# The second layer's matmul groups held in written order, with thirds of the output product between products of one PSUM bank

## The chip, the cores and the metric

The kernel runs on one core of a Trainium2 chip. The metric is the device time of one execution in microseconds (us). A core has five engines that run side by side, each with its own queue of instructions: TensorE (PE in the profile, its weight loads PEld), VectorE (DVE), ScalarE (ACT), GpSimd (POOL) and SyncE (SP), which here issues the DMAs. Matmuls write to PSUM, which is divided into banks; VectorE and ScalarE read the results there.

## The reference, cut to what matters

The whole program is an attention over packed keys and two feed-forward layers. The change touches the second layer alone:

```
g = x @ w_gate                       # x: 4608 x 512, w_gate: 512 x 1536
silu = g * (1 / (1 + exp(-g)))
val = x @ w_val                      # w_val: 512 x 1536
out = (silu * val) @ w_out           # w_out: 1536 x 512
```

All of it is in 32-bit floats; the kernel multiplies in the format float32r and takes three matmuls in place of one.

## The kernel before, in words

**Three matmuls for one.** Every operand is split into a high part and a low part. The helper `mm3` (line 284) adds low x high (line 287), high x high (line 288) and high x low (line 289) into one PSUM bank. So all of the matmuls in question carry these three line numbers, and the tile names tell them apart.

**Tiling of the second layer.** The 4608 tokens are cut into six blocks of 768 (`s`), each of two halves of 384 (`t`). The 1536 inner columns are cut into twelve pieces (`f`). One step `n` does one piece for one block, `n = 12 s + f`, so there are 72 steps. Within a step the two halves of gate and value (four blocks of results) come from seven products in place of eight, in Strassen's manner (`product`, line 894, `k` = 0 to 6). Each takes a sum or difference of input blocks (`xs2`, tiles `xA` and `xS`) against one of weight blocks (`gvw`, tile `gv`), with two `mm3` of 384 columns: six matmuls.

**The banks.** `gv_step` (line 913) uses the tags `h` and `at`, each with two banks: product 0 and 2 go to `xb`, 1, 3 and 5 to `yb`, 4 and 6 to `vb`. Products 0 and 2 add up in one bank, as do 4 and 6, and 1, 3 and 5; between them an engine reads the bank as it then stands. Line 928 copies product 0 to `p1` on ScalarE; `add` (line 911, VectorE) forms `u2`, `u3` and a new `p1`. Lines 932 and 933 make silu for half t=0 (ScalarE, VectorE); lines 948 and 949 make it for half t=1 (ScalarE, GpSimd). Lines 952 (VectorE, t=0) and 954 (GpSimd, t=1) multiply by the value.

**The output product.** `halves` (line 971) splits each result into `ph` (ScalarE, line 973) and `pl` (GpSimd, line 975). `out_unit(n, t)` (line 980) multiplies them by a piece of `w_out`. It does so in three groups of 128 tokens (`g`), each one `mm3` of 512 columns into a bank of its own: three matmuls, a third of the unit. Six banks (`acc0` to `acc3`, one of `h`, one of `at`) gather the output over the twelve steps of a block, which leaves `xb` with `vb`, and all `yb`, one bank each for most of a block. The first matmul of each third takes `pl` as its weights, the other two `ph`. At f = 11 the six banks are copied out (lines 995 and 997) and sent to memory, through a buffer that is also the buffer of the sums of the next block's inputs (`sums_x`, line 826, and `split_x`, line 835).

**What sets the order.** The kernel is written as one sequence; in it `out_unit` of step n-1 is called from within step n, through `between(0)` ahead of product 4 and `between(1)` at the step's end. The language's scheduler then runs through a simulated timeline and queues, on each engine, whatever is ready first by its own costs; where two are ready, what is written earlier. Dependences on tiles and banks are kept by semaphores. So the order of PE's queue before the change is the scheduler's, not that of the text. `tc.issue_after(ins)` (already used in lines 211, 630 and 635, outside of this layer) makes every instruction traced inside it, on the engine of `ins`, stand behind `ins` in that engine's queue; it adds no semaphore.

**Block changes.** In the last step of a block the inputs of the next are split into high and low parts (ScalarE line 856, VectorE lines 857, 840 and 846); loads (line 816), sums (lines 832 and 833) and the weight loads `load_gv` (line 873, SP) are hoisted by the scheduler as early as their buffers allow.

Of the kernel before, what the change touches and what calls it, by code (L numbers as in the profile page):

```python
# [8 lines left out]
F32 = mybir.dt.float32  # L9
F32R = mybir.dt.float32r  # L10
U32 = mybir.dt.uint32
AF = mybir.ActivationFunctionType
# [5 lines left out]
P = 128  # L18
T = 384
# [82 lines left out]
def tile_kernel(  # L102
# [21 lines left out]
    nc = tc.nc  # L124
    B, H, S, D = q.shape
    NP = p.shape[2]
    NT, DM = out.shape
    KC = DM // P
    NF1 = alpha.shape[0] // P
    NF2 = w_out2.shape[0] // P  # L130
# [6 lines left out]
    NBLK = NT // (2 * T)  # L137
# [4 lines left out]
    ps = ctx.enter_context(tc.tile_pool(name="ps", bufs=1, space=PSUM))  # L142
# [3 lines left out]
    vp = ctx.enter_context(tc.tile_pool(name="v", bufs=1))  # L146
# [137 lines left out]
    def mm3(o, wts, xs, start, stop, **kw):  # L284
        whi, wlo = wts
        xhi, xlo = xs
        nc.tensor.matmul(o, wlo, xhi, start=start, stop=False, **kw)  # L287
        nc.tensor.matmul(o, whi, xhi, start=False, stop=False, **kw)  # L288
        nc.tensor.matmul(o, whi, xlo, start=False, stop=stop, **kw)  # L289

    ident = sm.tile([P, P], F32, name="ident")
    make_identity(nc, ident)
# [300 lines left out]
    for f in range(NF1):  # L593
# [10 lines left out]
        c=quad(2, natural=True),  # L604
# [37 lines left out]
    def at(it, late, fn):  # L642

        plan.setdefault((it, late), []).append(fn)
# [157 lines left out]
        at(NB1 + 8 * j + 6, 0, lambda j=j: load_part(j))  # L802


    raw2, xs2, gvw, wo2, ps2, acc2 = {}, {}, {}, {}, {}, {}

    def load_x(s):
        for t in range(2):
            for c in range(KC):
                raw = utile("u", [P, T], f"xr{s}_{t}{c}")  # L810
                raw2[s, t, c] = raw
                a0 = t0 = (2 * s + t) * T
                while t0 < a0 + T:
                    j, c0 = divmod(t0, HS)
                    n = min(HS - c0, a0 + T - t0)
                    nc.sync.dma_start(
                        out=raw[:, t0 - a0 : t0 - a0 + n], in_=x1d[j][:, c, c0 : c0 + n]
                    )
                    t0 += n
# [15 lines left out]
    def split_x(s, name):  # L835

        if name == "S2":
            src = raws_of(s, "A11")
            for e in range(2):
                nc.vector.tensor_tensor(  # L840
                    out=src[e], in0=raw2[s, "S1"][e], in1=src[e], op=ALU.subtract
                )
        elif name == "S4":
            src = raws_of(s, "A12")
            for e in range(2):
                nc.vector.tensor_tensor(
                    out=src[e], in0=src[e], in1=raws_of(s, "A11")[e], op=ALU.subtract
                )
        elif name == "S3":
            src = raws_of(s, "A21")  # L850
        else:
            src = raw2[s, "S1"] if name == "S1" else raws_of(s, name)
        tag = X_TAGS[name]
        x = wpool.tile([P, 2, 2, T], F32R, tag=tag, name=f"x{name}_{s}", bufs=WBUFS[tag])
        for e in range(2):
            nc.scalar.activation(out=x[:, 0, e], in_=src[e], func=AF.Copy)
            nc.vector.tensor_tensor(out=x[:, 1, e], in0=src[e], in1=f32(x[:, 0, e]), op=ALU.subtract)
        xs2[s, name] = x
# [5 lines left out]
    def load_gv(n):  # L864
        if n >= NBLK * NF2:
            return
        f = n % NF2
        gvw[n] = [
            wpool.tile([P, 7, 2 * P], F32R, tag="C", name=f"gv{n}_{t}", bufs=WBUFS["C"])
            for t in range(2)  # L870
        ]
        for t in range(2):
            nc.sync.dma_start(out=f32(gvw[n][t]), in_=wgvd[f][:, t])

    def load_wo2(i):
        w = wpool.tile([P, 2, 2, 512], F32R, tag="B", name=f"wp{i}", bufs=WBUFS["B"])
        for e in range(2):
            wo2[2 * i + e] = w[:, e, 0], w[:, e, 1]
            nc.sync.dma_start(out=f32(w[:, e]), in_=wo2d[2 * i + e])

    for n in ("load", "A11", "S", "S2", "A22", "A12", "S4", "S3", "S1"):
        fn = dict(load=lambda: load_x(0), S=lambda: sums_x(0)).get(
            n, lambda n=n: split_x(0, n)
# [7 lines left out]
    for i in range(2, NF2 // 2):  # L891
        at(N1, 1, lambda i=i: load_wo2(i))

    def product(bank, n, k, start):

        s = n // NF2
        x = xs2[s, PRODUCTS[k]]
        hi, lo = gvw[n]
        for e in range(2):
            c = slice(e * P, (e + 1) * P)  # L900
            mm3(
                bank,
                (hi[:, k, c], lo[:, k, c]),
                (x[:, 0, e], x[:, 1, e]),
                start and e == 0,
                e == 1,
                skip_group_check=True,
            )

    def add(out, bank, x):  # L910
        nc.vector.tensor_tensor(out=out, in0=bank, in1=x, op=ALU.add)  # L911

    def gv_step(n, between):


        s, f = divmod(n, NF2)
        p1, u2, u3, s1, s2 = (
            gp2.tile([P, T], F32, tag=t, name=f"{t}_{n}", bufs=b)
            for t, b in (("p1", 2), ("u2", 2), ("u3", 2), ("s1", 1), ("s2", 1))
        )  # L920
        more = f == NF2 - 1 and s + 1 < NBLK

        def bank(tag, name):
            return ps.tile([P, 512], F32, tag=tag, name=f"{name}{n}", bufs=2)[:, :T]

        xb, yb = bank("h", "xb"), bank("at", "yb")
        product(xb, n, 0, True)
        nc.scalar.activation(out=p1, in_=xb, func=AF.Copy)  # L928
        product(yb, n, 1, True)
        add(u2, yb, p1)  # L930
        product(xb, n, 2, False)
        nc.scalar.activation(out=s1, in_=xb, func=AF.Sigmoid)  # L932
        nc.vector.tensor_tensor(out=s1, in0=xb, in1=s1, op=ALU.mult)  # L933
        product(yb, n, 3, False)
        add(u3, yb, p1)
        if more:
            split_x(s + 1, "S2")
        between(0)
        xb = bank("h", "vb")
        product(xb, n, 4, True)  # L940
        add(u3, xb, u3)
        if more:
            split_x(s + 1, "A12")
        product(yb, n, 5, False)
        add(p1, yb, p1)
        if more:
            split_x(s + 1, "S3")
        nc.scalar.activation(out=s2, in_=p1, func=AF.Sigmoid)  # L948
        nc.gpsimd.tensor_tensor(out=s2, in0=s2, in1=p1, op=ALU.mult)  # L949
        product(xb, n, 6, False)  # L950
        add(u2, xb, u2)
        nc.vector.tensor_tensor(out=s1, in0=s1, in1=u2, op=ALU.mult)  # L952
        halves(n, 0, s1)
        nc.gpsimd.tensor_tensor(out=s2, in0=s2, in1=u3, op=ALU.mult)
        halves(n, 1, s2)
        between(1)
        if more:
            for name in ("S1", "A22", "S4"):
                split_x(s + 1, name)
        load_gv(n + 2)  # L960
        if s + 1 < NBLK:
            if f == 5:
                load_x(s + 1)
            elif f == 8:
                sums_x_after(s + 1)

    def sums_x_after(s):
        split_x(s, "A11")
        sums_x(s)

    def halves(n, t, x):
        hi = utile("a", [P, T], f"ph{n}_{t}", F32R)
        nc.scalar.activation(out=hi, in_=x, func=AF.Copy)  # L973
        lo = utile("a", [P, T], f"pl{n}_{t}", F32R)
        nc.gpsimd.tensor_tensor(out=lo, in0=x, in1=f32(hi), op=ALU.subtract)  # L975
        ps2[n, t] = hi, lo

    ACC = ("acc0", "acc1", "acc2"), ("acc3", "h", "at")

    def out_unit(n, t):  # L980
        s, f = divmod(n, NF2)
        phi, plo = ps2.pop((n, t))
        for g in range(T // P):
            if f == 0:
                tag = ACC[t][g]
                acc2[t, g] = ps.tile(
                    [P, 512], F32, tag=tag, name=f"o{t}{g}_{s}", bufs=2 if tag in ("h", "at") else 1
                )
            c = slice(g * P, (g + 1) * P)
            mm3(acc2[t, g], (phi[:, c], plo[:, c]), wo2[f], f == 0, f == NF2 - 1)  # L990
        if f == NF2 - 1:
            o = vp.tile([P, T // P, DM], F32, tag="v", name=f"os{s}_{t}")
            for g in range(T // P):
                if g % 2:
                    nc.vector.tensor_copy(out=o[:, g], in_=acc2[t, g])
                else:
                    nc.scalar.activation(out=o[:, g], in_=acc2[t, g], func=AF.Copy)
            r0 = (2 * s + t) * T
            nc.sync.dma_start(
                out=out[r0 : r0 + T, :].rearrange("(g p) d -> p g d", p=P), in_=o  # L1000
            )
# [13 lines left out]
    gp1.close()  # L1015
    gp2 = ctx.enter_context(tc.tile_pool(name="g2", bufs=1))
    for n in range(NBLK * NF2):
        gv_step(n, lambda t, n=n: out_unit(n - 1, t) if n else None)
    for t in range(2):
        out_unit(NBLK * NF2 - 1, t)  # L1020


# [35 lines left out]
```

## Time and profile before

| | |
|---|---|
| median of 3 runs | 1809.73 us (1809.26 to 1810.11) |
| the profiled execution | 1811.54 us, its span 1809.8 us |
| mean granted TensorE clock | 0.978 of full speed |
| second layer, first product to last output matmul | from 863 us (879 for product 0) to 1802.6 us of the span |

The profile takes one execution: every instruction with its start and duration, and for idle time before it the instruction that ended the wait. The span runs from the first to the last instruction; the execution takes 1.7 us more than that. Durations of matmuls overlap, since they are pipelined, so the distance from one start to the next is the measure of a matmul's cost.

### The profile page before, as it was taken

How to read it: one execution, taken by the hardware profiler on the slowest of the kernel's cores; microseconds unless marked ns; L12 is line 12 of the kernel's file. 1: busy time of each engine (PE TensorE's matmuls, PEld its weight loads, DVE VectorE, ACT ScalarE, POOL GpSimd, SP SyncE). 2: the span in 40 equal slices, each digit the busy share in tenths (PEclk: the TensorE clock that was granted, in tenths of full speed). 3: DMA queues.
4: the chain of work that ended last, by engine and by line, in shares of the span. 5: the costliest groups of instructions: out<-in, count | busy, mean ns of one | idle time of the engine just before them, and what ended most of it. 6: DMA issues, size and time to landing. Idle time of an engine off the chain costs nothing.

```text
span 1809.8 us, 27262 instructions
## 1 busy us (share of the span) xinstructions
PE 1688.2 (93%) x10048; PEld 1481.4 (82%) x10048; DVE 1045.6 (58%) x1875; ACT 606.3 (34%) x1384; POOL 790.7 (44%) x824
## 2 busy tenths in 40 slices
PE   6698899999999999999999999999998999999997
PEld 3577689888887888889988888888887888888886
DVE  7999877776868677764533533443353354335332
ACT  5765543433434344332212311222231232113121
POOL 3666756555555656433323333333323333333232
PEclk7799999999999999999999999999998999999999
DMA  9333365544455455421734543454453445345342
GB/s 239 109 105 123 105 188 154 148 128 120 131 141 140 126 154 139 120 78 41 266 125 163 185 170 133 166 179 163 151 204 122 163 160 195 134 151 180 140 163 76
DMA packets 227750, 266.04 MB, mean 147 GB/s; under 512 B 130848, under 2 KB 190240, under 8 KB 227616
## 3 DMA queue, kind: packets, MB, share of 16 engines
q1 hardware_dynamic: 227616, 264.30, 45.7%
q8 instruction: 79, 1.29, 0.3%
q14 instruction: 55, 0.45, 0.1%
HBM read 214.70 MB, written 49.55 MB: 146 GB/s over the span
## 4 chain that ended last, share of the span: by engine, by line
PE 56%; DVE 14%; DMA 8%; issue 8%; POOL 6%; ACT 5%; SPq 1%; POOLq 0%; ACTq 0%; DVEq 0%
PE o L288 5%; PE o L289 5%; PE o L287 5%; PE acc L287 4%; PE acc L289 4%; PE acc L288 4%; DVE s L952 3%; DMA wgvd<-cva 3%; PE yb L287 3%; PE yb L289 3%; PE yb L288 3%; PE vb L289 3%; PE vb L287 2%; PE vb L288 2%; PE xb L287 2%
## 5 line engine op out<-in xcount | busy, mean ns | idle before, releaser
L949 POOL TENSOR_TENSOR s<-s,p 128x384 f32<-128x384 f32 x72 | 75.4, 1048 | 562.6 <-ACT s L948 562.6
L772 POOL TENSOR_TENSOR lo<-g,hi 128x288 fp32r<-128x288 f32 x256 | 224.0, 877 | 222.1 <-ACT hi L770 181.8
L911 DVE TENSOR_TENSOR u<-vb,u 128x384 f32<-128x384 f32 x144 | 80.2, 557 | 296.1 <-PE vb L289 295.9
L770 ACT ACTIVATE hi<-g 128x288 fp32r<-128x288 f32 x256 | 112.8, 441 | 257.5 <-DVE g L762 177.5
L948 ACT ACTIVATE s<-p 128x384 f32<-128x384 f32 x72 | 37.7, 524 | 443.9 <-DVE p L911 443.9
L287 PE MATMUL o<-wp,pl 128*128 128x512 f32 x432 | 171.5, 397 | 3.5 <-POOL pl L975 3.5
L288 PE MATMUL o<-wp,ph 128*128 128x512 f32 x432 | 172.6, 400 | 0.0
L289 PE MATMUL o<-wp,ph 128*128 128x512 f32 x432 | 172.5, 399 | 0.0
L287 PE MATMUL h<-a2h,ppw 128*128 128x288 f32 x512 | 159.1, 311 | 8.8 <-DVE ppw L587 5.2
L287 PE MATMUL xb<-xA,gv 128*128 128x384 f32 x288 | 107.0, 372 | 48.8 <-ACT p L928 39.9
L289 PE MATMUL h<-a2l,ppw 128*128 128x288 f32 x512 | 152.3, 298 | 0.0
L288 PE MATMUL h<-a2h,ppw 128*128 128x288 f32 x512 | 151.9, 297 | 0.0
L975 POOL TENSOR_TENSOR pl<-s,ph 128x384 fp32r<-128x384 f32 x144 | 144.3, 1019 | 15.8 <-ACT ph L973 14.7
L759 DVE TENSOR_SCALAR g<-h,al 128x288 f32<-128x288 f32 x208 | 105.7, 509 | 78.7 <-PE h L289 66.2
L287 PEld LDWEIGHTS h<-a2h,ppw 128*128 128x128 f32 x512 | 96.9, 189 | 40.1 <-DVE g L762 10.1
L911 DVE TENSOR_TENSOR u<-yb,p 128x384 f32<-128x384 f32 x144 | 79.5, 552 | 81.6 <-ACT p L928 65.9
L287 PEld LDWEIGHTS xb<-xA,gv 128*128 128x128 f32 x288 | 55.5, 193 | 72.6 <-ACT p L928 61.0
L973 ACT ACTIVATE ph<-s 128x384 fp32r<-128x384 f32 x144 | 74.8, 523 | 109.7 <-DVE s L952 105.5
L287 PE MATMUL yb<-xS,gv 128*128 128x384 f32 x288 | 98.2, 341 | 5.5 <-DVE u L911 4.2
L289 PEld LDWEIGHTS h<-a2l,ppw 128*128 128x128 f32 x512 | 96.7, 189 | 3.8 <-issue 3.8
L289 PE MATMUL xb<-xA,gv 128*128 128x384 f32 x288 | 99.6, 346 | 0.0
L933 DVE TENSOR_TENSOR s<-xb,s 128x384 f32<-128x384 f32 x72 | 40.1, 557 | 102.7 <-ACT s L932 102.7
(184 smaller groups left out, 4888.1 us busy)
## 6 DMA issues: line engine op xcount, KB each, us to landing
gv<-wgvd SPq DMA_DIRECT2D x144, 896.0 KB, 6.2
wgvd<-cva SPq DMA_DIRECT2D x84, 256.0 KB, 2.6
cva<-in_moe_w_out_dram SPq DMA_DIRECT2D x28, 512.0 KB, 3.7
v<-in_v_dram SPq DMA_DIRECT2D x16, 576.0 KB, 5.3
out_dram<-os SPq DMA_DIRECT2D x12, 768.0 KB, 3.8
cva<-in_moe_w_in_dram SPq DMA_DIRECT2D x16, 512.0 KB, 3.7
kr<-in_k_dram SPq DMA_DIRECT2D x96, 72.0 KB, 2.7
qr<-in_q_dram SPq DMA_DIRECT2D x96, 72.0 KB, 2.4
```

The lines of the kernel that those rows point to most:

```text
L287: nc.tensor.matmul(o, wlo, xhi, start=start, stop=False, **kw)
L288: nc.tensor.matmul(o, whi, xhi, start=False, stop=False, **kw)
L289: nc.tensor.matmul(o, whi, xlo, start=False, stop=stop, **kw)
L759: nc.vector.tensor_scalar(out=g32, in0=hp, scalar1=0.0, scalar2=al[:, f : f + 1], op0=ALU.min, op1=ALU.mult)
L770: nc.scalar.activation(out=hi, in_=x, func=AF.Copy)
L772: nc.gpsimd.tensor_tensor(out=lo, in0=x, in1=f32(hi), op=ALU.subtract)
L911: nc.vector.tensor_tensor(out=out, in0=bank, in1=x, op=ALU.add)
L933: nc.vector.tensor_tensor(out=s1, in0=xb, in1=s1, op=ALU.mult)
L949: nc.gpsimd.tensor_tensor(out=s2, in0=s2, in1=p1, op=ALU.mult)
L952: nc.vector.tensor_tensor(out=s1, in0=s1, in1=u2, op=ALU.mult)
L973: nc.scalar.activation(out=hi, in_=x, func=AF.Copy)
L975: nc.gpsimd.tensor_tensor(out=lo, in0=x, in1=f32(hi), op=ALU.subtract)
```

## The change

`product` and the thirds of the output product are traced inside `behind()`, which queues their matmuls behind the last matmul of the group traced before them. PE's order in the second layer is thereby that of the text. `out_unit` now does one third (`g`) at a call, and the calls are spread: one third of half t=0 stands between product 1 and 2, two behind product 3; one third of half t=1 stands between product 5 and 6, two behind product 6. Each third copies its own bank out at f = 11.

```diff
     def mm3(o, wts, xs, start, stop, **kw):
...
-        nc.tensor.matmul(o, whi, xlo, start=False, stop=stop, **kw)
+        return nc.tensor.matmul(o, whi, xlo, start=False, stop=stop, **kw)
...
+    before = []
+    def behind():
+        return tc.issue_after(before[-1].ins) if before else ExitStack()
     def product(bank, n, k, start):
...
-        for e in range(2):
-            c = slice(e * P, (e + 1) * P)
-            mm3(
...
+        with behind():
+            for e in range(2):
+                c = slice(e * P, (e + 1) * P)
+                last = mm3(
...
+        before[:] = [last]
...
         add(u2, yb, p1)
+        between(0, 0)
         product(xb, n, 2, False)
...
-        between(0)
+        between(0, 1)
+        between(0, 2)
         xb = bank("h", "vb")
         product(xb, n, 4, True)
...
         nc.gpsimd.tensor_tensor(out=s2, in0=s2, in1=p1, op=ALU.mult)
+        between(1, 0)
         product(xb, n, 6, False)
...
-        between(1)
+        between(1, 1)
+        between(1, 2)
...
-    def out_unit(n, t):
+    def out_unit(n, t, g):
...
-        for g in range(T // P):
...
+        with behind():
+            last = mm3(acc2[t, g], (phi[:, c], plo[:, c]), wo2[f], f == 0, f == NF2 - 1)
+        before[:] = [last]
+        if f < NF2 - 1:
+            return
+        if g == 0:
+            outs[t] = vp.tile([P, T // P, DM], F32, tag="v", name=f"os{s}_{t}")
+        o = outs[t]
+        if g % 2:
+            nc.vector.tensor_copy(out=o[:, g], in_=acc2[t, g])
+        else:
+            nc.scalar.activation(out=o[:, g], in_=acc2[t, g], func=AF.Copy)
+        if g == T // P - 1:
             r0 = (2 * s + t) * T
             nc.sync.dma_start(
...
-        gv_step(n, lambda t, n=n: out_unit(n - 1, t) if n else None)
+        gv_step(n, lambda t, g, n=n: out_unit(n - 1, t, g) if n else None)
     for t in range(2):
-        out_unit(NBLK * NF2 - 1, t)
+        for g in range(T // P):
+            out_unit(NBLK * NF2 - 1, t, g)
```

## Rows read from the trace of the kernel before

**Rows 1.** The page's first part: engine, busy us, share of the span, instructions.

```profile
PE 1688.2 (93%) x10048; PEld 1481.4 (82%) x10048; DVE 1045.6 (58%) x1875; ACT 606.3 (34%) x1384; POOL 790.7 (44%) x824
```

**Rows 2.** Waits of PE, 889 to 1794 us: total us, times, longest.

```profile
PE xb L287 <- ACT p L928: 39.9, 64, 2.0
```

**Rows 3.** Stretches: length; busy PE, PEld, DVE, ACT, POOL; clock, DMA share, GB/s.

```profile
912.22:1010.55 98.33, 93.67 (x481) 85.16 (x481) 34.41 (x56) 19.26 (x40) 33.19 (x32) 1.00 0.41 150
1669.00:1791.90 122.90, 117.08 (x601) 106.45 (x601) 43.01 (x70) 24.08 (x50) 41.48 (x40) 1.00 0.37 135
...
1318.70:1376.60 57.90, 51.81 (x242) 45.58 (x242) 30.98 (x50) 17.96 (x38) 19.69 (x18) 0.91 0.53 182
1628.90:1669.00 40.10, 36.69 (x182) 33.50 (x182) 23.10 (x37) 14.46 (x31) 13.13 (x12) 0.96 0.50 177
1010.55:1037.07 26.52, 24.26 (x121) 21.18 (x121) 19.08 (x31) 11.99 (x26) 8.68 (x8) 1.00 0.67 228
1037.07:1048.50 11.43, 11.43 (x62) 10.69 (x61) 5.03 (x10) 3.53 (x7) 4.38 (x5) 1.00 0.68 229
1048.50:1066.03 17.53, 14.82 (x61) 12.88 (x61) 6.88 (x10) 2.44 (x5) 6.62 (x6) 0.81 0.29 106
```

**Rows 4.** Timeline of a regular step: start us, us, engine, line, operation, tiles.

```profile
1402.04 0.33 PE L289 MATMUL vb<-xS,gv 128*128 128x384 f32 x1
...
1402.41 0.56 DVE L911 TENSOR_TENSOR u<-vb,u 128x384 f32<-128x384 f32 x1 [0.48 <-PE vb L289]
...
1402.62 1.01 POOL L949 TENSOR_TENSOR s<-s,p 128x384 f32<-128x384 f32 x1 [8.06 <-ACT s L948]
...
1403.00 1.05 DVE L952 TENSOR_TENSOR s<-s,u 128x384 f32<-128x384 f32 x1
...
1403.71 1.20 POOL L954 TENSOR_TENSOR s<-s,u 128x384 f32<-128x384 f32 x1
...
1404.08 0.52 ACT L973 ACTIVATE ph<-s 128x384 fp32r<-128x384 f32 x1 [1.54 <-DVE s L952]
1404.12 0.34 PE L289 MATMUL xb<-xA,gv 128*128 128x384 f32 x1
1404.51 0.47 ACT L928 ACTIVATE p<-xb 128x384 f32<-128x384 f32 x1
1404.88 1.98 POOL L975 TENSOR_TENSOR pl<-s,ph 128x384 fp32r<-128x384 f32 x2
...
1405.04 0.44 PE L287 MATMUL xb<-xA,gv 128*128 128x384 f32 x1 [0.58 <-ACT p L928]
...
1406.99 0.56 DVE L933 TENSOR_TENSOR s<-xb,s 128x384 f32<-128x384 f32 x1 [1.42 <-ACT s L932]
...
1407.25 0.39 PE L287 MATMUL o<-wp,pl 128*128 128x512 f32 x1
...
1411.37 0.33 PE L287 MATMUL vb<-xS,gv 128*128 128x384 f32 x1
...
1412.44 0.33 PE L287 MATMUL yb<-xA,gv 128*128 128x384 f32 x1
...
1413.48 0.33 PE L287 MATMUL vb<-xS,gv 128*128 128x384 f32 x1
```

**Rows 5.** Timeline of VectorE and GpSimd at two places of the first layer.

```profile
276.82 0.65 DVE L239 SCALAR_TENSOR_TENSOR cva<-cva 128x512 f32<-128x512 uint32 x1
276.82 1.31 POOL L772 TENSOR_TENSOR lo<-g,hi 128x288 fp32r<-128x288 f32 x1 [1.60 <-ACT hi L770]
597.52 1.31 DVE L239 SCALAR_TENSOR_TENSOR cva<-cva 128x512 f32<-128x512 uint32 x1
597.48 0.81 POOL L772 TENSOR_TENSOR lo<-g,hi 128x288 fp32r<-128x288 f32 x1 [1.55 <-ACT hi L770]
```

**Rows 6.** Timeline of VectorE at a block change, and of PE at the end.

```profile
1049.73 2.62 DVE L840 TENSOR_TENSOR xr<-xs,xr 128x384 f32<-128x384 f32 x2 [0.44 <-POOL xr L833]
...
1796.62 0.50 PE L287 MATMUL o<-wp,pl 128*128 128x512 f32 x1 [3.51 <-POOL pl L975]
```

More of the change, by code (lines that the diff above doesn't have):

```diff
@@ L802, in tile_kernel @@
         at(NB1 + 8 * j + 6, 0, lambda j=j: load_part(j))
-    raw2, xs2, gvw, wo2, ps2, acc2 = {}, {}, {}, {}, {}, {}
+    raw2, xs2, gvw, wo2, ps2, acc2, outs = {}, {}, {}, {}, {}, {}, {}
     def load_x(s):
@@ L898, in product @@
         hi, lo = gvw[n]
-        for e in range(2):
-            c = slice(e * P, (e + 1) * P)
-            mm3(
[L902 to L908, printed above, removed]
+        with behind():
+            for e in range(2):
+                c = slice(e * P, (e + 1) * P)
+                last = mm3(
+                    bank,
+                    (hi[:, k, c], lo[:, k, c]),
+                    (x[:, 0, e], x[:, 1, e]),
+                    start and e == 0,
+                    e == 1,
+                    skip_group_check=True,
+                )
+        before[:] = [last]
     def add(out, bank, x):
@@ L978, in tile_kernel @@
     ACC = ("acc0", "acc1", "acc2"), ("acc3", "h", "at")
-    def out_unit(n, t):
+    def out_unit(n, t, g):
         s, f = divmod(n, NF2)
-        phi, plo = ps2.pop((n, t))
-        for g in range(T // P):
[L984 to L997, printed above, removed]
+        phi, plo = ps2[n, t]
+        if f == 0:
+            tag = ACC[t][g]
+            acc2[t, g] = ps.tile(
+                [P, 512], F32, tag=tag, name=f"o{t}{g}_{s}", bufs=2 if tag in ("h", "at") else 1
+            )
+        c = slice(g * P, (g + 1) * P)
+        with behind():
[11 more added lines that the diff above has]
+        if g == T // P - 1:
             r0 = (2 * s + t) * T
```

## The prediction

> **What bounds the kernel now.** I read the page first, then the waits of the second layer, the time by stretch, and last the order of instructions in one regular step. The page has TensorE (PE) busy for 93% of the span [rows 1]; that is a mean over stages, so what the change is worth has to be read from the second layer. There the longest total that PE waits for is line 928, ScalarE's copy of a product out of its PSUM bank: 64 waits, 39.9 us of idle matmul time [rows 2]. By stretch, eight regular steps take 98.33 us and ten take 122.90, so one takes 12.29 us [rows 3]. Five stretches of eight steps and one of ten look like this: 50 regular steps. Between them lie four block changes of four steps each, three of 55.5 us (26.52 + 11.43 + 17.53) and one of 57.90, and a last change of three steps, 40.10 us [rows 3]. One step of each change takes 11.43 us with PE busy throughout, so that is a step without a wait in the old order.
>
> The timeline of a regular step shows where the other 0.86 us goes [rows 4]. The scheduler has put the next step's product 1 ahead of its product 0, so products 0 and 2, which share bank xb, stand next to each other. Product 0's last matmul starts at 1404.12, the copy of line 928 takes 0.47 from 1404.51, and product 2 starts at 1405.04: 0.92 instead of the usual 0.17. All six thirds of the output product run together from 1407.25 to 1411.37.
>
> **The change part by part.** The arithmetic is the same: 42 product matmuls and 18 output matmuls a step, the same copies, adds and DMAs. The edges force PE into the written order: 0, 1, third, 2, 3, two thirds, 4, 5, third, 6, two thirds.
>
> *The PE work of a step.* A product takes 1.04 us (1412.44 to 1413.48) and 1.07 behind output matmuls (1411.37 to 1412.44); a third is 4.12/6 = 0.69 [rows 4]. There are four switches from thirds to products in place of one: 7 x 1.04 + 4.12 + 4 x 0.03 = 11.52. I add 0.05 for switching into the thirds, which happens four times too and has no row of its own (0 to 0.1): 11.57.
>
> *The bank waits that go.* Product 2 now starts 1.04 + 0.69 us after product 0 has ended, and the copy needs 0.92 - 0.17 = 0.75 of it: hidden, with 1.0 to spare. Product 4 (same bank) needs the sigmoid and the multiply of line 933, which ended at 1407.55, 2.51 after product 2's start [rows 4]; in the new order 1.07 + 1.04 + 1.37 = 3.48 lie there. Product 6 and the next product 0 wait for one VectorE add each (0.56 plus some 0.45 of hand-over, from 1402.04 to 1402.97 [rows 4]); 1.7 and 1.4 us of PE work lie there. No bank wait is left in a regular step.
>
> *The wait that is late next.* The first third of step n-1 now stands two products into step n, and its first matmul needs `pl`, the low half of product t=0, which comes last in a chain that starts with product 6. Counted from product 6's last matmul (1402.04 = 0) the chain was: add 0.37 to 0.93, multiply of line 952 0.96 to 2.01, high half on ScalarE 2.04 to 2.56, then GpSimd's two subtractions from 2.84, held by its line 954 until 2.87, some 0.99 each, so `pl` at 3.83 [rows 4]. PE wants to load it at 0.17 + 1.37 + 1.07 + 1.04 - 0.17 = 3.48. Unchanged, the chain would hold PE for 0.4. But it moves: a third (0.72 with its switch) now stands between product 5 and product 6, so GpSimd's lines 949 and 954, which hang on product 5, come 0.72 earlier against product 6. Line 949 then ends at 0.87, and line 954 starts at 0.95, within 0.02 us of the multiply on VectorE at 0.96. Before, the multiply met line 949 already running and took 1.05; it ended 0.42 after 949 did.
>
> So what two such instructions do that start together decides the step. Where they start together (276.82) VectorE's took 0.65 and GpSimd's 1.31; where GpSimd's was 0.04 ahead it took 0.81 and VectorE's 1.31 [rows 5]: one runs whole and the other waits, and in a tie VectorE wins. The multiply then takes some 0.56 (0.96 to 1.52); line 954 ends some 0.87 later, 2.39 (0.86 was left of it after the multiply, 1404.05 to 1404.91 [rows 4]), the high half has long been there, `pl` at about 3.45 to 3.5, and PE waits 0.03. I take 11.60 a step. If GpSimd wins, line 954 ends at 1.97, the multiply 0.42 later at 2.39, the high half at 2.93, `pl` at 4.0, and PE waits 0.55: 12.12.
>
> The Trainium skill, "SBUF — State Buffer", section "Who interferes with whom", says that a VectorE instruction with two SBUF inputs contends with a GpSimd one that reads SBUF, and that issue order decides who blocks. By that rule taken strictly GpSimd, which is due 0.01 us earlier, holds the port and the step is 12.12. The trace agrees on the lock, but in its tie VectorE won.
>
> Regular steps: 50 x (12.29 - 11.60) = 34.5 us gained.
>
> *Block changes.* In two steps of each, VectorE also splits the next block's inputs (19.08 us busy in 26.52) and they cost 26.52 - 2 x 12.29 = 1.94 more than regular ones [rows 3]. That VectorE queue stays; I keep 1.94. The fourth step takes 17.53, 5.24 over a regular one, at a granted clock of 0.81 in the mean between the two levels 1.2 and 2.4 GHz [rows 3]: line 840's 2.62 us (1049.73) stands ahead of the add of line 911 that frees the bank for the next product 0 [rows 6], and a bank wait follows. In the new order two thirds behind product 6 cover 0.5 of that delay and the second wait is gone; the delay still reaches `pl`. So between 2.1 and 5.24 (plus the 2.4 by which the longest change exceeds the others, should DMAs land worse); I take 4.0. A change: 4 x 11.60 + 1.94 + 4.0 = 52.3, the four 209.4 against 224.4: 15.0 gained. The last change, with half of its remaining excess (40.10 - 36.01 - 1.94 = 2.15) kept: 34.8 + 1.94 + 1.1 = 37.8, 2.3 gained.
>
> *Ends.* At the end PE sits idle 3.51 us for `pl` [rows 6]; two thirds now lie inside: 1.4 gained. At the start, step 1 has no thirds behind product 6 to cover the same chain, and the products can no longer be shuffled among the first layer's last matmuls: 2 lost (0 to 4). Evacuations and the output DMA are the same instructions, issued a third at a time on engines with room; the second output DMA of a block moves to the end of its step, behind the same weight loads on SP. Its landing releases the buffer that the sums in front of line 840 wait for; that is in the bounds above.
>
> Sum: 34.5 + 15.0 + 2.3 + 1.4 - 2 = 51.2 from the profiled execution's 1811.54 is 1760.3. The median of the runs lies 1.8 lower (1809.73): 1758.5, told as 1759.
>
> **Rivals.**
> 1. GpSimd wins the tie: 12.12 a step. 50 x 0.17 = 8.5; changes 4 x 12.12 + 5.94 = 54.4, 6.7 gained; ends -1: 14 gained, 1796. For it: the calculated 0.01 us and the skill's rule. Against it: the tie in rows 5. 15%.
> 2. Clean block changes: with thirds between the products, line 840's delay falls into covered time. Changes 46.4 + 1.94, 31 gained in place of 15, the last 1 more, no loss at the start: 1738. Against it: 2.6 us exceeds any cover. 10%.
> 3. Rigid order at the changes: before, the scheduler could slip other matmuls ahead of a late product; now all of PE stands behind the product that waits for a split. If each change costs 60 us, it gives 16 back in place of gaining 15: 1790. For it: 19.08 of 26.52 us busy on VectorE. 13%.
> 4. Slower: the scheduler, whose line 954 comes 0.72 earlier too, queues the t=1 half before the t=0 half on GpSimd. Then `pl` comes one subtraction and a wait later, at 5.0, and PE waits 1.5: 13.1 a step, 50 x 0.8 = 40 lost, changes 9 lost: about 1860. It turns slower once PE's wait exceeds 12.29 - 11.57 = 0.72. Against it: the multiply is due 0.9 us before line 954 ends. 6%.
> 5. The skill's "TensorE: Matmul & The Clock Gate", section "A second HAM failure mode: psum-queue depth-cycling", tells of matmuls that cycle through banks losing the clock. If thirteen changes of bank a step in place of twelve did that, the step would near twice 11.6 and the kernel lose hundreds of us. The regular steps have a clock of 1.00 with twelve and a gap of 0.75 us [rows 3], and the gap goes. 1%.
>
> **How the numbers follow.** My case holds 55%. Its own spread is some 10 us each way (the fourth step's 2.1 to 7.6, the start). The range reaches to rivals 1 and 2: 1738 to 1797. A measurement tells 0.2%, 3.6 us, from no change. Faster: my case, rivals 1 and 2, most of 3: 0.89; same: 0.03; slower: rivals 4 and 5 and a rest of 3: 0.08.
>
> **What would show it.** Right: a regular step of 11.6 us with no PE wait on line 928; the multiply of line 952 at 0.56 and line 954 near 1.35; product 0 ahead of product 1 in each step; changes of 50 to 54 us. Wrong: line 287's output matmul waiting on line 975 in every step (rival 1 at 0.55, rival 4 at 1.5), or more than 56 us a change (rival 3).

## The result, and the profile after

| | before | after |
|---|---|---|
| median of 4 runs each, side by side | 1809.92 us (1809.26 to 1813.84) | 1761.35 us (1757.90 to 1764.65) |
| span of the profiled execution | 1809.8 us | 1760.6 us |
| mean granted TensorE clock | 0.978 | 0.985 |

The ratio is 0.9727, with an interval of 0.9703 to 0.9751. The forecast was 1759 us.

In the time by parts further down, and in the steps of the experiments, a step is counted from the start of its product 5 to the start of the next step's product 5. The stretches of [rows 3] begin with a product 6, and the stretches of the kernel after, shown below, with a product 4; a regular step is as long either way.

The page after, as [rows 1]: engine, busy us, share, instructions; and the group of a third's first matmuls, whose last columns are the idle time before them and who ended it.

```profile
PE 1669.6 (95%) x10048; PEld 1474.1 (84%) x10048; DVE 1019.8 (58%) x1875; ACT 606.4 (34%) x1384; POOL 797.9 (45%) x824
...
L287 PE MATMUL o<-wp,pl 128*128 128x512 f32 x432 | 171.6, 397 | 16.1 <-POOL pl L988 15.7
```

The waits of PE after, from 889 to 1745 us of the span (total us, times, longest), which answer to [rows 2]. Line 919 is the `add` that was line 911.

```profile
PE o L287 <- POOL pl L988: 13.4, 19, 1.9
PE xb L287 <- DVE u L919: 6.3, 4, 1.6
PE vb L287 <- DVE u L919: 1.1, 4, 0.5
```

The 39.9 us behind the bank's copy are gone without a rest. What is late next is `pl`, as forecast, but not in every step: 19 times, with up to 1.9 us.

The stretches after, with the columns of [rows 3]: eight regular steps, a change, a longer change, the last change, the second and the fourth step of the first change, and two regular steps that follow one another.

```profile
911.08:1004.24 93.16, 92.59 (x482) 85.58 (x481) 32.25 (x56) 19.36 (x40) 34.45 (x32) 1.00 0.43 159
1004.24:1055.72 51.48, 47.73 (x241) 42.37 (x240) 28.95 (x50) 17.78 (x38) 19.93 (x18) 1.00 0.60 204
...
1148.33:1201.49 53.16, 49.27 (x242) 43.91 (x240) 29.05 (x50) 17.74 (x38) 19.84 (x18) 0.97 0.58 198
1584.80:1621.34 36.54, 35.42 (x181) 31.88 (x180) 21.30 (x37) 14.57 (x31) 12.71 (x12) 1.00 0.53 194
1015.75:1030.10 14.35, 12.42 (x62) 10.48 (x61) 10.39 (x20) 5.67 (x12) 4.74 (x4) 1.00 0.76 239
1041.60:1055.72 14.12, 12.29 (x61) 10.50 (x60) 7.65 (x11) 2.33 (x5) 6.39 (x6) 1.00 0.43 159
1236.01:1248.07 12.06, 11.77 (x62) 10.67 (x60) 4.68 (x7) 2.33 (x5) 4.02 (x4) 1.00 0.41 153
1248.07:1259.57 11.50, 11.50 (x61) 10.71 (x60) 3.81 (x7) 2.45 (x5) 4.40 (x4) 1.00 0.44 161
```

The last two rows are the finding: a regular step takes 11.50 with PE busy throughout, or 12.06, and nothing between. The timeline of these two steps (columns as in [rows 4]), first the long one, then the short one:

```profile
1239.68 0.33 PE L289 MATMUL vb<-xS,gv 128*128 128x384 f32 x1
...
1240.64 1.02 POOL L966 TENSOR_TENSOR s<-s,u 128x384 f32<-128x384 f32 x1
1240.64 1.43 DVE L964 TENSOR_TENSOR s<-s,u 128x384 f32<-128x384 f32 x1
...
1242.11 0.94 ACT L986 ACTIVATE ph<-s 128x384 fp32r<-128x384 f32 x2 [2.64 <-DVE s L964]
...
1242.71 1.99 POOL L988 TENSOR_TENSOR pl<-s,ph 128x384 fp32r<-128x384 f32 x2 [1.05 <-ACT ph L986]
...
1243.15 0.34 PE L289 MATMUL yb<-xS,gv 128*128 128x384 f32 x1
...
1243.78 0.50 PE L287 MATMUL o<-wp,pl 128*128 128x512 f32 x1 [0.29 <-POOL pl L988]
...
1251.74 0.34 PE L289 MATMUL vb<-xS,gv 128*128 128x384 f32 x1
...
1252.70 1.44 POOL L966 TENSOR_TENSOR s<-s,u 128x384 f32<-128x384 f32 x1
1252.70 0.56 DVE L964 TENSOR_TENSOR s<-s,u 128x384 f32<-128x384 f32 x1
...
1254.10 1.98 POOL L988 TENSOR_TENSOR pl<-s,ph 128x384 fp32r<-128x384 f32 x2
...
1255.38 0.39 PE L287 MATMUL o<-wp,pl 128*128 128x512 f32 x1
```

Lines 966 and 964 are GpSimd's and VectorE's multiply by the value, the pair of the forecast's tie. Counted from product 6's last matmul, they start together at 0.96 in both steps. In the short one VectorE's takes 0.56 and GpSimd's waits (1.44); `pl` begins at 2.36 and is done 1 us later. In the long one GpSimd's runs whole (1.02) and VectorE's takes 1.43; `pl` begins at 3.03, and the first third starts 0.63 behind product 1's last matmul where 0.18 is usual, and its first matmul then holds the next one 0.33 instead of 0.23: 0.55 in all, which is 12.06 - 11.51.

In 61 of the 72 steps the pair starts within 6 ns of each other. Where GpSimd's start is at most 4 ns ahead, VectorE won every time; of the 27 where it is 5 or 6 ns ahead, GpSimd won 14, twelve of them in regular steps.

### The profile page after: what moved, and what is told of

It is laid out like the page before. It is cut to its first block, busy times and chain, and to the rows that moved or that the text cites. A ratio compares the mean times of both kernels' runs of the same rounds, so it can differ in the third digit from the quotient of the medians.

```text
span 1760.6 us, 27334 instructions
## 1 busy us (share of the span) xinstructions
PE 1669.6 (95%) x10048; PEld 1474.1 (84%) x10048; DVE 1019.8 (58%) x1875; ACT 606.4 (34%) x1384; POOL 797.9 (45%) x824
## 4 chain that ended last, share of the span: by engine, by line
PE 63%; DVE 10%; POOL 8%; DMA 7%; issue 7%; ACT 4%; SPq 1%; POOLq 0%; ACTq 0%; DVEq 0%
PE acc L287 5%; PE acc L289 5%; PE o L287 5%; PE acc L288 5%; PE o L288 4%; PE o L289 4%; PE yb L289 3%; PE yb L287 3%; PE yb L288 3%; DMA wgvd<-cva 3%; PE h L287 2%; PE xb L287 2%; PE xb L288 2%; PE xb L289 2%; PE vb L288 2%
## 5 line engine op out<-in xcount | busy, mean ns | idle before, releaser
L287 PEld LDWEIGHTS h<-a2h,ppw 128*128 128x128 f32 x512 | 96.8, 189 | 39.0 <-DVE g L762 10.4
L287 PEld LDWEIGHTS o<-wp,pl 128*128 128x128 f32 x432 | 81.7, 189 | 30.9 <-POOL pl L988 23.9
L287 PE MATMUL xb<-xA,gv 128*128 128x384 f32 x288 | 97.9, 340 | 6.7 <-DVE u L919 6.3
L287 PE MATMUL vb<-xS,gv 128*128 128x384 f32 x288 | 97.2, 338 | 1.1 <-DVE u L919 1.1
L288 PEld LDWEIGHTS h<-a2h,ppw 128*128 128x128 f32 x512 | 96.9, 189 | 1.4 <-issue 1.4
```

## The experiments

The theory: a step before had two waits for a PSUM bank that competed for one cover, that is, for other matmuls that fill the wait. Product 0 must wait about 0.8 us behind product 6 for VectorE's add, and product 2 needs 0.75 between product 0's end and its own start for the copy. The scheduler's order 6, 1, 0, 2 spends product 1 on the first and leaves the second open. The held order spends product 1 on the second and thirds on the first. The early first third then hangs on `pl`, and by that on the tie. The texts of the expectations call this theory A where it needs a name; their rivals stand in them. "Before" was run beside each group: 1812.89 us (15 runs) with `again`, `order_only`, `thirds_only` and `third_later` on one chip; 1812.88 (17) with `swap_only`, `tie_lost`, `changes_held` and `groups_of_three_held` on a second; 1813.38 (9) with the other three on a third.

**The changed kernel again** (`again`, no edit).

> The changed kernel once more, timed beside the others. In its first profile a step took either 11.51 us or 12.06 us, and line 966 (GpSimd) started between 6 ns before and 1 ns after the multiply of line 964 (VectorE). Theory (the tie sets the step): again only these two lengths, 11.51 where the multiply takes 0.56 and 12.06 where it takes 1.43, in another mixture, so that single runs spread by several us (1757.9 to 1764.7 so far) in units of 0.55; the median 1758 to 1765. Rival (something outside, such as DMA or the clock, lengthens some steps): lengths other than these two, or long steps with the multiply at 0.56.

Measured: 1755.1 us (1752.18 to 1759.95), ratio 0.9686 (0.9665 to 0.9707). Its profile has no step of 12.06: all regular stretches of eight are 92.05, 11.51 a step, though eleven pairs started 5 ns apart. Its 50 regular steps take 575.3 us, where those of the first profile take 582.0. So the number of lost ties varies from run to run, and with it a few us. It doesn't make up all of the scatter; runs of the kernel before, which has no such tie, spread by 10 us too (1807.97 to 1817.56).

**Order held, no third between products of one bank** (`order_only`). Three thirds go behind product 3 and three behind product 6.

```diff
-        between(0, 0)
         product(xb, n, 2, False)
 ...
+        between(0, 0)
         between(0, 1)
         between(0, 2)
 ...
-        between(1, 0)
         product(xb, n, 6, False)
 ...
+        between(1, 0)
         between(1, 1)
         between(1, 2)
```

> Order held as in the change, but the thirds back in two groups of three: 0, 1, 2, 3, three thirds, 4, 5, 6, three thirds. Theory A (it is the order 0, 1, 2 that hides line 937's copy, since product 1 alone is 1.04 us and the copy needs 0.75 of it; the thirds between the products aren't needed for the banks): no bank wait, the first third comes 6.4 us behind product 6 instead of 3.6, so that it waits for no pl however the tie falls: 11.45 us a step, no step of 12.06, total 1748 to 1756. Theory B (the thirds between products of one bank bring the gain): waits come back between 0 and 2, 2 and 4 or 4 and 6: over 11.9 us a step, total 1775 to 1810.

Measured: 1733.63 us (1730.10 to 1738.87), ratio 0.9568 (0.9546 to 0.9589), faster than the change by more than I expected. The waits of PE that are left, 889 to 1716 us:

```profile
PE vb L287 <- DVE u L919: 1.2, 3, 0.6
PE yb L287 <- DVE u L919: 1.1, 5, 0.2
PE xb L287 <- DVE u L919: 0.4, 1, 0.4
```

and a change, with the columns of [rows 3], takes 48.27 instead of 51.48:

```profile
1001.47:1049.74 48.27, 47.20 (x242) 42.63 (x242) 29.58 (x50) 17.87 (x38) 19.68 (x18) 1.00 0.64 218
```

So the thirds between products of one bank are not what gains. They cost 21.5 us (1755.1 against 1733.6 on the same chip). By the profiles of the two, 18.2 of 23.2 us come from the four changes (210.8 against 192.6), 0.6 from the regular steps and the last change, the rest from start and end. Since the first third now stands behind product 3, it finds `pl` ready even where VectorE is late: no wait for `pl` is in the list.

**Thirds alone** (`thirds_only`): the thirds as in the change, but no edges, so that the scheduler orders PE's queue as before.

```diff
-        return tc.issue_after(before[-1].ins) if before else ExitStack()
+        return ExitStack()
```

> The thirds called where the change calls them, but no edges: the scheduler orders TensorE's queue by its own simulated times. On its list the steps are again 1, 0, 2, 3, all six thirds, 4, 5, 6, as in the kernel before. Theory A (the held order brings all of it): 12.29 us a step with the wait on line 937 between products 0 and 2, total 1805 to 1815, the same as before. Theory B (calling the thirds one by one has an effect of its own): total under 1795.

Measured: 1812.61 us (1810.17 to 1815.44), ratio 1.0 (0.9987 to 1.0012). The waits of PE, 889 to 1794 us, against [rows 2]:

```profile
PE xb L287 <- ACT p L937: 40.0, 64, 2.0
```

The old wait is there, to a tenth. Where the text puts the thirds does nothing while the scheduler decides.

**Products 0 and 1 alone in order** (`swap_only`): one edge a step, product 1 behind product 0.

```diff
-        with behind():
+        with behind() if k == 1 else ExitStack():
 ...
-        before[:] = [last]
+        if k == 0:
+            before[:] = [last]
 ...
-        with behind():
+        with ExitStack():
             last = mm3(acc2[t, g], (phi[:, c], plo[:, c]), wo2[f], f == 0, f == NF2 - 1)
-        before[:] = [last]
```

> One edge a step and no more: product 1 is held behind product 0; all else of TensorE's queue is the scheduler's. Its list reads 0, 1, 2, three thirds, 3, three thirds, 4, 5, 6, and then at once the next 0. Theory (two bank waits a step compete for one cover: 6 to the next 0 needs about 0.8 us of other work, 0 to 2 needs 0.75, and product 1 can stand in one gap only, so thirds must stand in the other): the wait moves from between 0 and 2 to between 6 and 0, on the add of line 919; 12.2 to 12.3 us a step, total 1795 to 1815, no gain over the kernel before. Rival (the swap of products 0 and 1 was all that was wrong with the old order): 11.4 to 11.5 us a step, total 1725 to 1745.

Measured: 1808.32 us (1804.85 to 1814.37), ratio 0.9981 (0.9967 to 0.9995); 12.42 to 12.44 a step. The waits of PE, 889 to 1794 us; line 920 is `add`:

```profile
PE xb L287 <- DVE u L920: 51.2, 64, 3.4
```

There are 64 waits again, now between products 6 and 0 in place of 0 and 2, of 0.8 us in the mean. Two waits and one cover: this is what the theory rests on. The size of a step was expected a little lower, at 12.2 to 12.3. A regular step is longer than before (12.29); against that the four changes take 214.9 instead of 224.8, and the total hardly moves.

**The first third behind product 2** (`third_later`): `between(0, 0)` goes from ahead of product 2 to ahead of product 3.

> The change with one call moved: the first third stands behind product 2 instead of ahead of it (0, 1, 2, third, 3, two thirds, 4, ...), so that TensorE needs pl 1.04 us later. Theory (the only wait left in a regular step is that third's wait for pl when GpSimd wins the tie): the tie still falls both ways, but no step takes 12.06; every regular step 11.51 to 11.55, total 5 to 11 us under the changed kernel (1749 to 1757), and single runs within 2 us of each other. Rival (the tie isn't the cause of the long steps): the same mixture and spread as the changed kernel, total within 3 us of it.

Measured: 1744.88 us (1742.94 to 1746.89), ratio 0.9627 (0.9610 to 0.9644). Regular steps 11.51, changes 49.9 to 50.7. In its profile GpSimd won none of the near ties, so it says nothing on what a lost one costs; the gain on `again` comes from the four changes (201.5 against 210.8). I had expected runs within 2 us of each other, if ties made the scatter; they spread by 4.

**The tie made certain** (`tie_lost`): a copy of one column on VectorE delays its multiply; GpSimd must win.

```diff
         add(u2, xb, u2)
+        nc.vector.tensor_copy(out=u2[:, :1], in_=u2[:, :1])
         nc.vector.tensor_tensor(out=s1, in0=s1, in1=u2, op=ALU.mult)
```

> The changed kernel with a copy of one column of u2 onto itself on VectorE between the last add and the multiply, so that the multiply comes some 0.06 to 0.1 us later; the result stays what it was. Theory (whichever of the two starts first runs whole, the other waits it out): GpSimd's line now wins in every step, the multiply takes 1.3 to 1.4, and every regular step is 12.06 us whatever the length of the copy: total 1778 to 1792, 25 to 33 us over the changed kernel for an instruction of under 0.1 us. Rival (no lock: the copy costs its own length at most): 11.51 to 11.6 a step, total within 7 us of the changed kernel.

Measured: 1788.57 us (1785.24 to 1790.40), ratio 0.9867 (0.9847 to 0.9887). Of the 50 regular steps 49 take 12.05 to 12.07. In the one left VectorE's multiply started 0.085 us ahead of GpSimd's in spite of the copy, ran whole (0.56), and the step took 11.57. The timeline of a long one, then the waits of PE, 889 to 1770 us:

```profile
1067.69 0.15 DVE L964 COPY u<-u 128x1 f32<-128x1 f32 x1
1067.70 1.02 POOL L967 TENSOR_TENSOR s<-s,u 128x384 f32<-128x384 f32 x1
1067.88 1.25 DVE L965 TENSOR_TENSOR s<-s,u 128x384 f32<-128x384 f32 x1
```

```profile
PE o L287 <- POOL pl L989: 28.4, 66, 2.0
```

An instruction of 0.15 us costs the kernel 33 us against `again` (other chip, befores equal to 0.01), 27.5 of them in the regular steps of the two profiles. This is the forecast's rival 1 made real: 12.06 where it said 12.12, 1789 where it said 1796.

**The lost tie, covered** (`tie_lost_covered`): the same copy, and the first third behind product 2.

> The one-column copy on VectorE, by which GpSimd wins in every step (12.07 us a step without more), together with the first third behind product 2 instead of ahead of it. Theory (the lost tie costs time only because the first third then waits for pl): the multiply still takes 1.24 but pl is needed 1.04 us later, so every regular step is 11.51 again, total 1743 to 1751. Rival (a slow multiply holds TensorE by some other way too, such as the add of line 919 or the copy of line 937 behind it): steps of over 11.7, total 1760 to 1789.

Measured: 1766.89 us (1760.87 to 1769.91), ratio 0.9738 (0.9712 to 0.9763); steps of 11.78, not the 11.51 expected. The wait for `pl` went from 66 times to 5, but another took half its place. The timeline of ScalarE and PE:

```profile
955.97 0.94 ACT L987 ACTIVATE ph<-s 128x384 fp32r<-128x384 f32 x2 [2.65 <-DVE s L965]
956.81 0.48 ACT L937 ACTIVATE p<-xb 128x384 f32<-128x384 f32 x1
957.34 0.45 PE L287 MATMUL xb<-xA,gv 128*128 128x384 f32 x1
```

The late multiply delays the two high halves on ScalarE, the copy of product 0 stands behind them, and product 2, now without a third ahead of it, waits 0.27 for the copy. That the tie costs through `pl` is shown; that `pl` is its only way to PE was wrong.

**The changes held** (`changes_held`): the changed kernel, with VectorE's work for the next block tied to later places in its queue: the sums (line 832) behind the `add` of `u3` in the block's fifth step, the subtraction of S2 (line 840) behind that of the seventh, the splits of A22 and S4 behind the multiply of the last.

```diff
+            with tc.issue_after(mark[NF2 * s - NF2 + 4].ins) if s else ExitStack():
                 nc.vector.tensor_tensor(out=raw2[s, "S1"][e], in0=a21, in1=a22, op=ALU.add)
 ...
+                with tc.issue_after(mark[NF2 * s - NF2 + 6].ins) if s else ExitStack():
                     nc.vector.tensor_tensor(
 ...
-        add(u3, yb, p1)
+        mark[n] = add(u3, yb, p1)
 ...
+            with tc.issue_after(done.ins):     # done: the multiply of line 964
                 for name in ("A22", "S4"):
```

> The changed kernel with VectorE's work for the next block held in place: the sums behind the add into u3 of the block's fifth step, the first subtraction of S2 behind that of the seventh, the splits of A22 and S4 behind the multiply of the last step. Theory (a block change loses its time because such work is queued ahead of an add or of the multiply on which TensorE waits, not because VectorE has too much to do): the steps of 14.3 to 15.9 and 14.1 to 15.5 us fall to 11.5 to 12.3; four changes give 4 to 6 us each, the last 1: total 1730 to 1740 against 1755 to 1761. Rival (VectorE has too much to do at a change, wherever it stands): the same loss shows in other steps; total within 6 us of the changed kernel.

Measured: 1735.97 us (1735.31 to 1737.26), ratio 0.9580 (0.9562 to 0.9598). A change takes 47.9 to 48.4; its fourth step falls from 14.1 to 11.51, its second only to 13.4. The timeline of the changed kernel shows both causes; its last row is the wait at the end of the span, which is taken up further down:

```profile
1021.47 2.19 DVE L857 TENSOR_TENSOR xS<-xr,xS 128x384 fp32r<-128x384 f32 x2
...
1023.58 0.54 DVE L964 TENSOR_TENSOR s<-s,u 128x384 f32<-128x384 f32 x1
...
1025.80 0.50 PE L287 MATMUL o<-wp,pl 128*128 128x512 f32 x1 [1.84 <-POOL pl L988]
...
1046.07 2.39 DVE L840 TENSOR_TENSOR xr<-xs,xr 128x384 f32<-128x384 f32 x2
...
1048.38 0.55 DVE L919 TENSOR_TENSOR u<-vb,u 128x384 f32<-128x384 f32 x1
...
1048.98 0.44 PE L287 MATMUL xb<-xA,gv 128*128 128x384 f32 x1 [1.57 <-DVE u L919]
...
1746.91 0.50 PE L287 MATMUL o<-wp,pl 128*128 128x512 f32 x1 [2.34 <-POOL pl L988]
```

Two splits of 2.19 stand ahead of the multiply, and `pl` and the first third come 1.84 late; two subtractions of 2.39 stand ahead of the add that frees product 0's bank, and PE waits 1.57. That these are the causes is shown for the fourth step, which loses its whole excess with the hold, and in part for the second.

**Both together** (`groups_of_three_held`): the order of `order_only` with all three holds.

> Both findings together: order held, thirds in two groups of three (0, 1, 2, 3, three thirds, 4, 5, 6, three thirds), and VectorE's work for the next block held in place as in the run beside this one. The kernel with the groups of three alone took 1733.6 us, with changes of 47.8 to 48.7 us for four steps of 11.50. Theory (what is left of a change is work queued ahead of the adds): changes of 46 to 46.6, total 1723 to 1729. Rival (VectorE's load): no gain, 1731 to 1738.

Measured: 1743.29 us (1738.58 to 1744.11), ratio 0.9614 (0.9594 to 0.9634): slower than `order_only`, a miss. Three of the four changes take 50.3, of which the second step 15.27, and one takes 48.95, with a second step of 13.76. The timeline of VectorE in the first of them:

```profile
1018.73 1.37 DVE L966 TENSOR_TENSOR s<-s,u 128x384 f32<-128x384 f32 x1
1020.02 2.65 DVE L859 TENSOR_TENSOR xA<-xr,xA 128x384 fp32r<-128x384 f32 x2
1022.60 1.82 DVE L848 TENSOR_TENSOR xr<-xr,xr 128x384 f32<-128x384 f32 x2
1024.34 0.54 DVE L922 TENSOR_TENSOR u<-yb,p 128x384 f32<-128x384 f32 x1
```

The splits held behind the multiply now stand ahead of the next step's first add, and product 3, which needs its bank, waits some 2.1 us. In the three long steps the granted clock is 0.89, in the short one 1.00, so about 1.5 us of each is a lower clock and not the wait itself. A held instruction doesn't vanish; it delays what comes behind its new place.

**Only the hold that worked** (`three_sums_held`): `order_only` with the first two holds, without the one on the splits; and `order_only` a second time beside it (`order_again`).

> The order held with the thirds in two groups of three, and of VectorE's work for the next block only the sums and the first subtraction of S2 held in place (behind the add into u3 of the fifth and the seventh step); the splits stay where the scheduler puts them. Theory (holding the splits behind the multiply made the earlier run slower, by queueing them ahead of the add that product 3 waits for; holding the sums was a gain): the last step of a change falls from 12.4 to 12.9 to 11.5, the others stay: 3 to 6 us under the kernel beside it, 1726 to 1732. Rival (the hold of the sums was what cost time): 1738 to 1745.

> The order held with the thirds in two groups of three, once more, timed beside the next: 1730 to 1739, regular steps of 11.50.

Measured: 1729.40 us (1728.71 to 1732.99), ratio 0.9539 (0.9519 to 0.9559), against 1736.28 (1734.96 to 1738.40), ratio 0.9575 (0.9555 to 0.9594). This is the fastest version, 26 us below `again` (other chip, befores 0.5 apart) and 32 below the first measurement of the change. A change (columns of [rows 3]) takes 46.86, all four alike, of which four steps without any wait would take 46.0; then the one wait of PE that lasts, 889 to 1712 us:

```profile
1003.55:1050.41 46.86, 46.56 (x241) 42.78 (x241) 26.48 (x46) 18.09 (x38) 17.12 (x16) 1.00 0.68 225
```

```profile
PE yb L287 <- DVE u L922: 1.0, 5, 0.2
```

## Why the prediction was right, and where its sizes were off

The time by parts of the two profiled spans, in us gained:

| part | forecast | measured | from |
|---|---|---|---|
| 50 regular steps | 34.5 | 32.8 | 614.8 to 582.0 |
| four changes | 15.0 | 15.2 | 224.8 to 209.6 |
| last change | 2.3 | 3.5 | 40.07 to 36.54 |
| end | 1.4 | 0.6 | 18.89 to 20.39, with three thirds (2.07) more inside |
| start | -2 | -3.0 | 0.94 later, with three thirds (2.07) fewer done |
| sum | 51.2 | 49.2 | spans 1809.8 to 1760.6 |

**The bank waits.** Right: all 64 are gone [rows 2], with no wait between product 2 and product 4. `thirds_only` shows that the new places of the thirds do nothing without the held order, `swap_only` that product 0 ahead of product 1 alone only moves the wait, `order_only` that the held order does it without any third between products of one bank. There product 1 alone covers product 0's copy, so the third beside it, which the forecast counted into the cover, isn't needed; where it stands it makes the first third early and the tie costly.

**PE's work in a step.** 11.50 where I said 11.57: the eight switches between products and thirds cost 0.10 in all (11.50 less 7 x 1.04 and 4.12), where I put 0.17. That gives 3.3 us back over 50 steps.

**The tie.** The mechanism was right, down to the start at 0.96 and the two ends: 0.03 of wait where VectorE wins (none measured) and 0.55 where GpSimd does (0.55 measured). The forecast that VectorE wins held in 38 of 50 regular steps of this profile, in all of them in `again`. Twelve lost ties took 12 x 0.55 = 6.6 us. I gave rival 1 a chance for all steps at once; it comes step by step. That the regular steps came near the forecast (32.8 for 34.5) is partly luck: a step without a lost tie is 0.1 shorter than my 11.60, some 5 us over 50 steps, and the lost ties took 6.6 back. `again`, the same kernel, with no lost tie in the regular steps of its profile, took 1755.1.

The Trainium skill, "SBUF — State Buffer", section "Who interferes with whom", has issue order decide who blocks, and by that GpSimd should have won each near tie in which it started first. Of those it lost all 21 with a lead of 1 to 4 ns, won 10 of 23 with one of 5 ns and all 4 with one of 6 ns. Whether the starts in the profile tell the order of issue to the nanosecond, no run here shows.

**The changes.** The sum was right by two errors that cancel. I gave the fourth step 4.0 over a regular one; it has 2.6 to 3.0. Its clock stays at 1.00 where it was 0.81, and PE is busy for 12.29 in it instead of 14.82 [rows 3]; the wait behind line 840 that I reckoned with is still there, 1.57. I gave the first two 1.94 together; they have 2.8 to 4.4. In all four changes the first third waits 1.8 for `pl` behind two splits on VectorE, a place that I had not looked at. In two of them the granted clock then falls too, and the same step takes 1.54 more; the columns are those of [rows 3]:

```profile
1161.03:1176.77 15.74, 13.79 (x61) 12.14 (x61) 9.51 (x17) 6.24 (x13) 4.64 (x4) 0.89 0.64 206
1306.79:1320.99 14.20, 12.25 (x61) 10.59 (x61) 9.40 (x17) 6.24 (x13) 4.26 (x4) 1.00 0.71 233
```

Rival 2's clean change (48.34) is what `changes_held` reaches (47.9 to 48.4), and its 1738 us with it (1736), but only with edits that the change doesn't have. (Added up again, rival 2's terms give 1739.5, not 1738; nothing else hangs on it.)

**The ends.** The start lost 3.0 rather than 2: step 1's first third waits 1.64 for `pl`, the cause that I named; for the other 1.4 the runs show no cause. At the end PE waits 2.34 instead of 3.51 [rows 6]; the last multiply lost its tie too, and `pl` came 4.05 behind product 6 instead of 3.85. From that wait's end to the end of the span it takes 13.70 instead of 13.14: the granted clock of the first 2 us behind it is 0.71 instead of 0.88, and the first output DMA is issued 4.17 behind it instead of 3.60.

**The rivals.** Rigid order at the changes (3) did not happen: 51.5 to 53.5 us, not 60. No regular step has the wait of 1.5 that the t=1 half queued first would give (4). The clock fell nowhere in regular steps, which have 1.00 with thirteen changes of bank (5).

**What stays open.** What decides a pair that starts 5 ns apart: in one profile VectorE lost 10 of 23, in two others (`again`, `third_later`) none of 11 and none of 12. And how much of the 4 to 10 us between runs of one kernel is the tie, since kernels without it scatter as much; a lower clock behind a wait at a block change, which the same kernel shows in two changes of one profile and in one of the other, is 1.5 us each time. Why it falls in some changes and not in others, with the same wait of PE ahead of it, the runs don't show.

## What to carry to other kernels

Count the waits for a bank in a step, and the work that can stand in each: where two waits need a cover and the queue gives one, moving the cover moves the wait (`swap_only`), and only an order that covers both gains. Then look at what the reordered work itself needs, and put it where its input is early by more than the largest delay ahead of it; an order that just fits turns each small delay on another engine into idle time in every step. An instruction that is held back is paid for by what stands behind its new place, so hold those behind which nothing urgent comes.

## What the runs showed of the hardware

Two instructions of VectorE and GpSimd on SBUF tiles of 128x384 that start within a few ns of each other don't share: one runs whole (0.56 or 1.02), the other ends late (1.43 or 1.44). In three profiles (the change, `again`, `third_later`) GpSimd won none of the near ties in which it was ahead by 4 ns or less, 10 of 46 in which it was ahead by 5 ns, and all 4 in which it was ahead by 6; ahead by 0.19 us (`tie_lost`) it won all 56. VectorE's multiply ends about 0.41 behind GpSimd's when it loses. So a step's length has two values, 11.51 and 12.06, and which one it takes is decided within nanoseconds.
